# A gated mix of two attentions on one core: logits pieces of 512, 320, 320 and 128 columns in place of four of 320, a last Q part of 128 columns, a new order

## The chip, the core and the metric

The kernel runs on one core of one Trainium2 chip. Its five engines run at the same time and wait for each other by semaphores: TensorE (PE, matmuls, results into PSUM), VectorE (DVE), ScalarE (ACT), GpSimd (POOL) and SyncE (SP, which issues DMAs). PSUM has eight banks of 512 float32 columns on 128 partitions. The metric is the device time of the kernel in microseconds, lower is better.

## What is computed

The result is `g * a + (1 - g) * b`, with a gate `g` for each of 2,048 rows of x (512 columns, bfloat16).

```python
def _A_ref(x, mem0, Wq, Wk, Wv, Wo, seg_len):        # 32 heads of 128, seg_len 32, M = 8
    mem = mem0
    for s in range(n_seg):                           # 64 segments
        h = concatenate([mem, x[s * 32:(s + 1) * 32]])
        q, k, v = h @ Wq, h @ Wk, h @ Wv             # per head
        p = softmax(where(mask, q k^T * scale, -1e9))
        o = (p @ v) @ Wo
        mem = o[:, :M]                               # the next segment starts from it
        outs.append(o[:, M:])

def _B_ref(x, wq, wk, wv, wo, beta):                 # 32 heads of 16, 4 blocks of 512 rows
    for s in range(4):
        p = softmax(q[s] k[s]^T * scale + causal mask)
        o = sig(beta) * (phi(q[s]) M) / (phi(q[s]) z) + (1 - sig(beta)) * p @ v[s]
        M, z = M + phi(k[s])^T v[s], z + sum phi(k[s])
    return o @ wo

g = sigmoid((x * gate_w).sum(-1))
return g * _A_ref(...) + (1 - g) * _B_ref(...)
```

Attention A is a recurrence: the first eight output rows of a segment are the memory of the next one, so its 64 segments run one after the other. Attention B doesn't depend on A.

## The kernel before

**The whole.** The program first lists some 6,800 operations with their reads and writes and then lays them out on the engines. The order on each engine is written out: `ORDER` is a packed text that lists, for PE, ACT, DVE, POOL and SP, which operation comes when (`sequences`, L472; `given`, L396). Where an operation may run on one of two engines (copies out of PSUM on ACT or DVE, some products on DVE or POOL), the list on which it stands decides. Each operation's waits, and the PSUM banks that it gets, follow from the order.

**A segment of A** (`p_seg`, from L1444 on). The tokens and the memory, transposed, are projected with Wq, Wk and Wv (`wproj`, matmuls in L1422), each in two halves of 16 heads (r = 0 and 1). A projection's matmuls use all 128 rows of the array and 32 of its columns, so that four run side by side. Results are copied out of PSUM (`copy`, L1002), K and Q transposed on DVE (`ktr`, L1497). The second Q projection is made in two parts (`two`, L1555): a part's matmuls, its copy and its transposition follow each other. Then come the scores (L1512 and L1516; a mask matmul in L1029 before them), the exponential (L1521), the sums (L1536) and their reciprocals (L1540, L1542), the normalisation (L1544, L1546), and the value product of each half r (`f_pv`, L1577, and `f_pw`, L1586). A value product uses 32 rows and 128 columns of the array, four times side by side, and writes columns 0 to 159 of four PSUM banks, a *quad*. Copies take it to OT_sb, and Wo (L1314) makes the output rows and the memory of the next segment (DVE, L1332 to L1337). Rows whose result the next segment doesn't need are projected apart, four segments at once (`xr`, `rem_q`, `rem_k`, `rem_v`, `OTr_sb`), and fill TensorE between the steps of the recurrence.

**B in units.** B runs as 16 units, each of eight heads of a block of 512 rows, in two halves q = 0 and 1 of four heads. A half's logits, transposed and without the part above the diagonal, have 1,280 columns for each head: key blocks 0, 3, 1 and 2 with 512, 128, 384 and 256 columns, in that order (`COL`, L1123). They are made in four *pieces* of 320 columns (`PIECE`, L1125). A piece is one operation of TensorE (`p_logits`, matmuls in L1146, again 32 rows by 128 columns of the array, one matmul for each head and key block that it touches), two exponentials of ACT over two banks each (`p_exps`, L1164), and one mask of POOL over the 128 diagonal columns (L1170, `DIAG`). When all four pieces are done, the value product of B follows (L1187).

**Where the pieces stand.** From unit 3 on (`ALONE`), `plan` (L703) gives each of the 26 halves the segments between two rounded places of a straight line: they start in segments 1, 3, 5, 8, 10, 12, 15, 17, 20, 22, 24, 27, 29, 32, 34, 36, 39, 41, 43, 46, 48, 51, 53, 55, 58 and 60, and the last ends at 62. So 17 halves have two segments and nine have three. A piece either *rides*: it shares the quad of the second value product (r = 1) of a segment, in columns 160 to 479, and its matmuls come right before that product's (`carry`). Or it stands *alone*, with a quad of its own (`alone`, `p_piece`, L1193). Halves of two segments have two pieces alone, halves of three segments one. The pieces of units 0 to 2 all stand alone. A quad's banks are closed to others until all its copies and exponentials are done.

The lines that place them now:

```python
            for p, at in enumerate(((s - 0.3, s, s + 0.7, s + 1), (s, s + 0.7, s + 1, s + 2), (s, s + 1, s + 2, s + 3))[min(end - s, 4) - 2]):
                if at == int(at):
                    self.carry[int(at), 1] = (u, q, p)
                else:
                    self.alone.append((at, u, q, p))
```

Of the kernel before, what the change touches and what calls it, by code (L numbers as in the profile page):

```python
# [15 lines left out]
    "c-nPZ2|yIp8~@(U?#`aDpc0BE%HfgsomYk;kY(l-rCDN{VwqNIYMyCore%1Rnn!rynSz9h;(Z%lq-kEEsR;@!3(U@&|9i8?yczhf!tTy|^S$r*eZTK}Pd5Y_F;`It7Qt!M>jdXFZ"  # L16
    "o}-UlLQEyp%Znl@BL;{n;K2$&H>mTz4SFmT->}>Uj3k}Ax1#@|F)jy%a)CuJat}R+mVI0VSn<{jtTiAHr)-JHnVW?7+7^4Mjwxk0EEq7O){4P{F=1({YSvLVSQH!nLG4W_PiTg50"
    "2~?Cjevt%qpGqX9JTf2%N|n43{DSW=?CJH`$aW^l;(b7AT27at_>WV<G2E+e=NC_xT4})(%_O;1cK|@!%sMuR5FrosV`z$GZL-ngj8W-QHDeyQR&AmT>-AJX~r9w&EP<vf>k13>}"
    "YuMGWGzU!~8%&JQ-1f(c4LLI~N5IeQV0#?OF2!QE<RZ?L2efGsfP4iSf(uCn}cIN$12`{P+6F9gn+{LDZu1y+Cn%`e0KXaOQp5~=dwr?T)a2rjn0i#RdRP*D_60^lgLUW?-3T5AD"
    "jybi^^oj}%>U%zo>Jb8OZ<N}L1(=#JDDoS_`pkgh2B0%=U>r|~rbo`cqusO2TW~0a<WCe1=<RUh>xlYGAT@awnt*sMpDAF5er(SIgaCr*VEC!Gp!1GiZ{)5^AJm?7j_+?@1XVC66"  # L20
    "fK}v0dtnjOMt8&ES#TM#+-5CV24f)gF^mT=dd2_h7_tMPi`R}>Q*C+|IKc{F8M+b*CahBw{|@l86F&Jw<gJA$VEhbw5jb2flMdk9=>lxN@wK9KSIXHo05@sWTy_w|B0V@xG|X$k!"
    "5Qc(z>l4d0gO{L*8zySK|+AI=Yc|?i|A>-rv~5b&x$60G`~bF5g;`*UeUgp8#$P~WuO<H3;HrU6qp@?poi!G*1ZFJdo>Z@TR5FXf;4NkN4_;Q_>=tEN6g`@fLb1bpaQZOiBXA>+V"
    "H_fUo0j7tZRV`qWIE%l9QVe4i}WBen=dJJ$-3R$`vD)ECd(}i!6v}wbKMbU|KIybFj0I<yVs21`WWjcz74CIxX<zN6}V_>`=sknfI7Lom-iDQqlY4j3tj35S_u#NIL8@#(|@(^gD"
    "q0MO1`W<fvwgK|q|<WpWYQIAZErNVb+NA!hN)%6Z)m)oCLd#K2<P`G#<>Spirme1+>R!DTrEufjoS2e3LBmW(FSix)!Cv_)X{<k$nW+{BAwE4V<Gi@XNJ6qu-J|I%D~`W1pX(dr6"
    "(Zsdy$M1J#|UcaIjK_A87OP!BGmm~3{MiDW2`b1JS#zG4zYL8z&jn!$w&VgMtAR!PCfvr_vXm#I&D5^58Xr!WX?sD?;Wsu1EGvETU^t@Rm^QJ;WnomV`C2^nywC;mQ$Yfy?Ur|D_"
    "+x^7LIRr4fPb(%|7#Kycye@;J*805BKVblW2D^Y*GHwNd0uQboqwdro;&<wLP(!K-hDODb5;6!@=<%CuNDROMkMxyQ!@7G&;`g2uwoqyYIK2&-U4g}V{#iBP3SzT(=$yDIx0r};d"
    "Nfrr`}5L`NyOOQqQPFs*-F9YE_D=Av!#v~1t^1;Pt@?xMDN{1dK?MP(&QfgfDlfp4L48({ACl!_Z={bdSQl?kBP9gHeF!YDiZ}!fSaJ`F@)>OoG{{7l9QCr;5++xqT}nYJ(f%ef~"
    "c~)u+~#VO0>bU0*1m<2xW-kOk04bH`epzFFYc_HvHD-Ka11iv=>z?H<I=tQX?Qxb~61n`atq8hKl#IxN?r?i*2q4HEG5LAY^gk%flVv+w|Ack1N&eV+-P*$I%~$fqC(V=2F6+_tK"
    "`$8cX!18sAl7csb{#;Jk*=Paxt!Za1~P%cZhXN^zu1U15uA4^8D0gNtMmY~^4ON{QNWB&IM|jnZ6*Xhn-kCz4tQhr7rk=C+VQPuR<@C=B(ynW-%49~@;K9!UNyT@S$JF#tytozt5"
    "C5q%x@h_(LpPy`V@*Acw6w7TY-iq_!{C<tnj^Sg(%r<~diL6o##{=@EL37^jN263L+F9ox%n6xg^Gt&DDu=FUTEBz%LVBu$V;StF#Po6I_Sl#@!P^<e$H^}ZKKyE(N>>^7aeuavs"  # L30
    "k{{#SP{$7ig0u5Y#H#>}Wt<&{zDiRhT?0mtAHBEmPeKPL;WPxrHfu(gCf6ag`T(LL?1@J_fS6ROGaBXcH@L-8_<H^ipOtaX;r-0nFvbWeghvU(DST1;KExcXR$dh9w3HG@%d90<&"
    "ZW<b$c$)3=>3m_l&*Y%8{2^}?JvWB^OX~U;fkSdIUfR$4m;v2B`Bx%y#9>54MH3xB7MT$<H0T`m}T6&coXW6Tz;aqV#X!tpSC9S7t)}gBN}W{riGy>zgB*<TzR7uy-}OUuQyyO)-"
    "siOn$h@AL#ivGJ0EhjT1YoyYvW@MFLY>wp|);&Ib8AT;<D}gmu1TFWeRi2Xv>GoU=hpKt%IM&zyT+LjSMg{%J4pXZF;3H(_mrLFQqV+Mk!eItZb1NzWE}MK`K&_YyvM`A%AvKzYV"
    "6M0H<G6fTl+~AFZw|9zwo$KKdS=2?!i51O%%Fm0IS_mN~K|<SP-X20y3A9NgotFGgo9z#&ED)b^)HyWPWZdZABn)#r-7Kv>_;>|+c47YjIdg`vPoNGMcK=SH8l(t6$@=uwE7Cp>8"
    "J4G5f9fY3Gsdp_1c|2}SxF2o#+IoO!z`7&Dd$OV5rg4fas^_$65>v`>`tO75lLm)1OSd4-&iXHX_h^bH?qYv@SS-tpTj8@=i{0!Fx@dx;B>^y*$&Ibf2aaey?M-8ZvZ+2K906G;w"
    "WHuyZ#$|TBj5~wi3Yz~Vw*NjLKy;YPcpls)v}Wj_Jww``O8;rn?AhSbTfj}M4%p7)QNd<#1yT{P@4!jC%?t&m@28UsI&1?}pF;uNPRSB&F4OJ+^+iK~Symw&j*0|(Ke%>FY#=)BN"
    "0spfp&%?Kz=B6z9)ysf+03461+@^^-o}?i&M^U}c-C+77cFah+fy~TfT9r3H41Qh_k%GH?u0wY8qIIZc3Da0hh!jwt)LdMEzr%qwFd=0Yf$sPLpEI?83~L)1Ja1Ir4Am7O(Z5i7H"
    "sQrz;oYifr9W2n9Nw<l2@YM>RO+vTNqYiL!3<xQL)MTck{vq0&;jvo<Gh^0@8rGT41v2z;L1?*n+3d2;pr7mOweE(dIlIws*&e8XG)n-JF5!io%L><BK7Hv&ktcHjy~mb#d?~jV!"
    "hHj}G5V!QGw)64V9AOABTQzYPI(_@{P9>#MSPW`ymLx8jZ+ez)#j6d+sV=8A(zM$#eqPWZlF9-{?1D%y77{uvWcu*Wk2=1nIHIxroS<Q3gq^AiCitVL6|%S*}&loDNz?@|#Ovrg7"
    "tVs-B{y-BQ})dBi8M82qy(AlnBfoa~TlvstPHxaIbt8p>sJ>DE0b{9e41Ft?THB#-==UG!__3IXK+mmE1QP(Vx{pH-D1WKNm@Fcc2U4-G+QC{ppooCOXH7RU|H$SZ$i`v6)H=-7b"  # L40
    "VYu9TE#oa2e;Z&jsaRW&V{)EovUA||DA8f|LP&=Ln{Y%?&x_<KQD;2W0SBf{m_LaM<h6(5pzs2C2JQ12AqAhbglp-*#);na7n|lyhXr4N4HEHLgWwPD#SSD!HVDR{8{Tu6y*US{T"
    "kwLx);kMarJ>-i{{Z3k#8<PtesK_jfMBE~8$sYcJX(AOU-e^=7McSr$ZHXiS};|I!wb9Pdqj^{>_L5m!wW)1Ls6Lb%H0O&)dMxW-~+*eaNMm3PL2ezgRlUCx~tOTlSM@YAZOAy(+"
    "z^dU-Z??&t7;^!!dagxF)QSuheG>mt@P{{&6k&yP1Anj1uhzysfLXqOsecGwI$Kd#-IvuRHeD@OQnTYhdUyFp@WD)?z{RsFYnxlhNo;lcTNY6C1fJ96$HrHx0|rXq`8t&3>?OYX?"
# [93 lines left out]
class Slot(Res):  # L137
# [1510 lines left out]
```

## Time and profile before

| what | us |
|---|---|
| median of three runs | 815.55 (813.28 to 816.82) |
| the profiled execution | 813.89 |
| its span, first to last instruction | 811.9 |
| TensorE busy in the span | 788.2 |
| DVE, ACT, POOL busy | 643.7, 523.1, 257.8 |

How to read it: the span is what the profiler saw of one execution, and its own time lies 2.0 us above it. In the views, a line names the line of the program (L1146), the engine, the operation, the tiles it writes and reads (`pb` is PSUM), its size in partitions by elements, and a count (x4). PE is TensorE's matmuls, PEld its weight loads, which run beside them. Matmuls overlap, and their lengths are longer than the distance of their starts; what a piece of work costs TensorE is read from the start of one group to the start of the next. The mean granted clock of TensorE was 1.000.

### The profile page before, as it was taken

The numbers are of one execution on the slowest core, as the hardware profiler recorded it, in microseconds if no ns is written. First come the engines' busy times: TensorE is split into PE (matmuls) and PEld (weight loads), VectorE is DVE, ScalarE is ACT, GpSimd is POOL, SyncE is SP. The second block draws the span as 40 slices with busy tenths as digits, with TensorE's granted clock in tenths as the row PEclk, the third lists the DMA queues.
The fourth block names the chain that finished last, engine by engine and source line by source line (L and its number), as shares of the span: only waits on it lengthen the run. The fifth ranks groups of instructions, "written<-read, shape, count | busy, mean of one in ns | idle before, by whom it ended". The sixth has DMA issues, their size and how long they took to land.

```text
span 811.9 us, 51762 instructions
## 1 busy us (share of the span) xinstructions
PE 788.2 (97%) x23598; PEld 501.2 (62%) x23607; DVE 643.7 (79%) x1681; ACT 523.1 (64%) x1198; POOL 257.8 (32%) x564
## 2 busy tenths in 40 slices
PE   9899999999999999999999999999999999999987
PEld 4456666666666666666666665656766665666655
DVE  4878887788889787787787887786877898787886
ACT  4666656776666656767667666577666656766662
POOL 4542221233223332422422322333323223432440
PEclk9999999999999999999999999999999999999999
DMA  8983202121200111121011111100111010010001
GB/s 327 417 256 63 47 16 45 36 52 27 48 25 21 46 27 40 33 46 34 21 33 48 38 25 42 30 24 20 40 48 31 21 31 21 16 25 22 22 21 37
DMA packets 71696, 45.14 MB, mean 56 GB/s; under 512 B 50046, under 2 KB 69942, under 8 KB 69942
## 3 DMA queue, kind: packets, MB, share of 16 engines
q1 hardware_dynamic: 70422, 40.92, 17.8%
q8 instruction: 185, 3.03, 1.6%
q10 hardware_dynamic: 1056, 0.92, 0.4%
q14 instruction: 33, 0.27, 0.1%
HBM read 30.33 MB, written 8.87 MB: 48 GB/s over the span
## 4 chain that ended last, share of the span: by engine, by line
PE 84%; DVE 8%; DMA 3%; ACT 2%; issue 2%; SPq 1%; POOL 1%; DVEq 0%; POOLq 0%; ACTq 0%
PE pb L1422 46%; PE pb L1314 18%; PE pb L1029 6%; PE pb L1146 3%; PE pb L1187 2%; PE pb L1577 2%; DMA st<-in_gate_w_dram 2%; PE pb L1512 2%; PE pb L1536 1%; PE pb L1031 1%; DVE V_sb L1002 1%; PE pb L1586 1%; DVE st L1002 1%; PE pb L1235 1%; DVE QT_sb L1497 1%
## 5 line engine op out<-in xcount | busy, mean ns | idle before, releaser
L1164 ACT ACTIVATE PTB<-pb 128x640 bf16<-128x640 f32 x240 | 158.5, 705 | 41.0 <-PE pb L1146 29.8
L1002 ACT ACTIVATE st<-pb 128x512 bf16<-128x512 f32 (+2 forms) x232 | 112.9, 499 | 104.3 <-PE pb L1422 76.1
L1422 PE MATMUL pb<-Wv_sb,hT 128*32 128x512 bf16 x2048 | 152.5, 380 | 0.0
L1422 PE MATMUL pb<-Wq_sb,hT 128*32 128x256 bf16 (+1 forms) x3072 | 139.2, 308 | 0.3
L1314 PE MATMUL pb<-Wo_sb,OT_sb 128*32 128x256 bf16 x4096 | 130.8, 273 | 2.2 <-issue 1.8
L1422 PE MATMUL pb<-Wk_sb,hT 128*32 128x512 bf16 x2048 | 131.1, 379 | 1.2 <-issue 0.9
L1314 PEld LDWEIGHTS pb<-Wo_sb,OT_sb 128*32 128x32 bf16 x4096 | 102.3, 96 | 12.6 <-issue 2.3
L1170 POOL TENSOR_SCALAR_AFFINE_SELECT PTB<-PTB 128x512 bf16<-128x512 bf16 x120 | 77.7, 648 | 90.2 <-ACT PTB L1164 82.2
L1422 PEld LDWEIGHTS pb<-Wq_sb,hT 128*32 128x32 bf16 x3072 | 79.7, 97 | 42.4 <-DVE hT L1337 4.4
L1546 POOL TENSOR_TENSOR PT_sb<-PT_sb,rc_sb 128x64 bf16<-128x64 bf16 x81 | 28.9, 356 | 188.9 <-ACT rc_sb L1542 174.9
L1422 PEld LDWEIGHTS pb<-Wk_sb,hT 128*32 128x32 bf16 x2048 | 53.2, 97 | 49.6 <-DVE hT L1337 2.3
L1002 DVE CAST st<-pb 128x512 bf16<-128x512 f32 (+1 forms) x123 | 67.2, 549 | 15.4 <-PE pb L1422 12.7
L1002 ACT ACTIVATE OT_sb<-pb 128x320 bf16<-128x320 f32 (+1 forms) x139 | 57.4, 429 | 32.2 <-PE pb L1586 31.3
L1002 DVE CAST OT_sb<-pb 128x320 bf16<-128x320 f32 (+2 forms) x121 | 56.5, 475 | 18.5 <-PE pb L1586 17.6
L1002 DVE CAST V_sb<-pb 128x512 bf16<-128x512 f32 x90 | 61.5, 684 | 8.8 <-PE pb L1422 7.9
L1497 DVE STREAM_TRANSPOSE QT_sb<-st 128x128 f32<-128x128 f32 (+1 forms) x192 | 61.8, 335 | 8.3 <-ACT st L1002 6.4
L1540 ACT ACTIVATE rc_sb<-pb 128x160 f32<-128x160 f32 x128 | 38.9, 304 | 42.7 <-PE pb L1536 36.2
L1332 DVE STREAM_TRANSPOSE pb<-pb 128x256 f32<-128x256 f32 x63 | 29.3, 465 | 40.7 <-PE pb L1314 40.4
L1521 ACT ACTIVATE PT_sb<-pb 128x224 bf16<-128x224 f32 x128 | 45.5, 356 | 23.0 <-PE pb L1516 19.1
L1422 PEld LDWEIGHTS pb<-Wv_sb,hT 128*32 128x32 bf16 x2048 | 48.0, 97 | 20.0 <-ACT st L1002 0.7
L1497 DVE STREAM_TRANSPOSE KT_sb<-st 128x256 f32<-128x256 f32 x128 | 54.6, 427 | 7.0 <-ACT st L1002 5.5
L1544 DVE TENSOR_TENSOR PT_sb<-PT_sb,rc_sb 128x160 bf16<-128x160 bf16 x128 | 45.2, 353 | 8.9 <-ACT rc_sb L1542 7.3
(200 smaller groups left out, 1449.4 us busy)
## 6 DMA issues: line engine op xcount, KB each, us to landing
Wv_sb<-in_A_Wv_dram SPq DMA_DIRECT2D x4, 1024.0 KB, 11.2
Wk_sb<-in_A_Wk_dram SPq DMA_DIRECT2D x4, 1024.0 KB, 19.3
Wq_sb<-in_A_Wq_dram SPq DMA_DIRECT2D x4, 1024.0 KB, 26.6
Wo_sb<-in_A_Wo_dram SPq DMA_DIRECT2D x4, 1024.0 KB, 22.2
rest_v<-stg SPq DMA_DIRECT2D x112, 32.0 KB
rem_v<-rest_v SPq DMA_DIRECT2D x28, 128.0 KB, 2.5
a_rows<-ao SPq DMA_DIRECT2D x63, 32.0 KB
stg<-a_rows SPq DMA_DIRECT2D x15, 128.0 KB
```

Of the source, the lines that this page charges most:

```text
L1002: self.P.op(("act", "dve"), (lambda a: a.activation(dst, src(), ACT.Copy), lambda d: d.tensor_copy(dst, src())), reads=reads, writes=write ...
L1029: ins = pe.matmul(out[32 * c:32 * c + 32], lhsT[:, 32 * c:32 * c + 32], rhs, start=start, stop=stop, tile_position=(0, 32 * c), **kw)
L1164: P.op("act", (lambda dst=dst, src=src: lambda a: a.activation(dst, src(), ACT.Exp, scale=0.25))(), reads=[pair], writes=["%s%d_%d" % (nam ...
L1170: P.op("gp", (lambda pt=pt, ii=ii: (lambda g: g.affine_select(pt, pt, ([[0, len(ii)]] if len(ii) > 1 else []) + [[1, 128]], ALU.is_ge, 0.0 ...
L1314: ins = pe.matmul(pb[so.b][p0:p0 + 32, 0:256], tok(r, g, l), half(h, d, q), start=(r == 0 and g == 0 and l < 2), stop=(r == 1 and g == 3 a ...
L1332: P.op("dve", lambda d: d.transpose(pb[so.b][:, 256:512], pb[so.b][:, 0:256]), reads=[so], writes=[rt], name="turn%s" % name, cost=0.468, ...
L1422: ins = pe.matmul(self.pb[sl.b][32 * g:32 * g + 32, 0:hi - lo], x[:, c, 0:32], cols, start=(c == 0), stop=(c == C - 1), tile_position=(0, ...
L1497: op("dve", (lambda dst=dst, src=src: lambda d: d.transpose(dst, src))(), reads=["st%d%s" % (i, tag)], writes=["%sT%d%s" % (kind, r, tag)] ...
L1521: op("act", lambda a: a.activation(PT[:, r, :], pb[rb.b][:, 0:224], ACT.Exp, scale=SCALE), reads=[rb], writes=["PT%d" % r, "PT%dr" % r], n ...
L1540: op("act", lambda a: a.activation(rc[:, r, :], pb[rb.b][:, 0:160], ACT.Ln), reads=[rb], writes=[rr], name="ln%d_%d" % (s, r), cost=t_act( ...
L1544: op("dve", lambda d: d.tensor_tensor(mine[r], mine[r], by_head(rc[:, r, :]), ALU.mult), reads=[rp, rr], writes=[rp], name="nrm%d_%d" % (s ...
L1546: op(("dve", "gp"), tuple((lambda e: e.tensor_tensor(rest[r], rest[r], late(rc[:, r, :]), ALU.mult)) for _ in range(2)), reads=[rp + "r", rr],
```

## The change

Three things change.

First, the pieces. Their bounds now depend on how many segments the half has (`cut`). With two segments they are 0, 512, 640, 960 and 1,280, so pieces of 512, 128, 320 and 320 columns; with three segments 0, 352, 640, 960 and 1,280, so 352, 288, 320 and 320; otherwise four of 320. With two segments piece 0 (512 columns) stands alone ahead of segment s, piece 2 rides the second value product of s, piece 1 (128 columns) the first of s + 1 and piece 3 the second of s + 1. With three segments none stands alone: piece 0 (352) rides the second value product of s, piece 1 (288) the first of s + 1, piece 2 the second of s + 1 and piece 3 the second of s + 2. So 26 pieces fewer stand alone (17 in place of 43 from unit 3 on), and 26 first value products carry one. A piece of 352 columns fills its banks, 160 + 352 = 512.

Second, the second Q projection's parts are 384 and 128 columns in place of 256 and 256.

Third, `ORDER` is another text. Both texts list 6,790 operations: 2,979 on PE, 367 on SP; on ACT, DVE and POOL 1,203, 1,681 and 560 before and 1,177, 1,701 and 566 after.

```diff
-        self.carry, self.alone = {}, []
+        self.carry, self.alone, self.cut = {}, [], {}
...
-            for p, at in enumerate(((s - 0.3, s, s + 0.7, s + 1), (s, s + 0.7, s + 1, s + 2), (s, s + 1, s + 2, s + 3))[min(end - s, 4) - 2]):
-                if at == int(at):
-                    self.carry[int(at), 1] = (u, q, p)
-                else:
-                    self.alone.append((at, u, q, p))
+            self.cut[u, q] = k = min(end - s, 4) - 2
+            if not k:
+                self.alone.append((s - 0.3, u, q, 0))
+            for p, at in zip((0, 2, 1, 3), ((-1, 1, 2, 3), (1, 3, 2, 5), (1, 3, 5, 7))[k]):
+                if at > 0:
+                    self.carry[s + at // 2, at % 2] = (u, q, p)
...
-    PIECE = 320
+    PIECES = ((0, 512, 640, 960, 1280), (0, 352, 640, 960, 1280), (0, 320, 640, 960, 1280))
+
+    def piece(self, u, q, p):
+        at = self.PIECES[self.cut.get((u, q), 2)]
+        return at[p], at[p + 1]
...
-        P, pb, par, lo = self.P, self.pb, u % 2, self.PIECE * p
+        P, pb, par, (lo, hi) = self.P, self.pb, u % 2, self.piece(u, q, p)
...
-        parts = [(kc, max(lo, c0), min(lo + self.PIECE, c0 + 512 - 128 * kc)) for kc, c0 in self.COL.items()]
+        parts = [(kc, max(lo, c0), min(hi, c0 + 512 - 128 * kc)) for kc, c0 in self.COL.items()]
...
-        P, lo, n = self.P, self.PIECE * p, self.PIECE
+        P, (lo, hi) = self.P, self.piece(u, q, p)
+        n = hi - lo
...
-        two = ((0, 256), (256, 512))
+        two = ((0, 384), (384, 512))
```

More of the change, by code (lines that the diff above doesn't have):

```diff
@@ L20 @@
[L20 to L31, printed above, removed]
@@ L76 @@
[L76 to L79 removed]
+    "c-n1Q2S8Lu6P|t7xq~|dG1!QLC3Y-CVvAU?VTn;<iLrOZ5=+!*>@`ti#U72s-V0)HsMs|sQ4{^`6_9cV+`Zj@_r1G&<v@YEd%Lq!zWHWm*%HDR+I2ea6IZD7&kPvJ&7Q)I4shWGf"
@@ L1148, in f_l @@
             return ins
-        o = P.op("pe", f_l, reads=["KT8_%d" % par, "QTm" if q else "QT8_%d" % par], writes=slot.pairs, name="bL%d_%d" % (u, 4 * q + p), cost=0.15,
+        o = P.op("pe", f_l, reads=["KT8_%d" % par, "QTm" if q else "QT8_%d" % par], writes=slot.pairs, name="bL%d_%d" % (u, 4 * q + p), cost=0.017 + (hi - lo) / 2400,
                  prio=prio, mode="r32")
```

115 lines of the change are left out of this document (63 added, 52 removed).

## The prediction

> **What bounds the kernel now.** I read the page's busy shares first, then the shares of the chain of waits by engine, then the busy time of the stretch without start and end.
>
> ```profile
> span 811.9 us, 51762 instructions
> PE 788.2 (97%) x23598; PEld 501.2 (62%) x23607; DVE 643.7 (79%) x1681; ACT 523.1 (64%) x1198; POOL 257.8 (32%) x564
> ...
> PE 84%; DVE 8%; DMA 3%; ACT 2%; issue 2%; SPq 1%; POOL 1%; DVEq 0%; POOLq 0%; ACTq 0%
> ```
>
> ```profile
> 68.00:780.00 712.00, 700.31 (x21618) 452.07 (x21614) 574.43 (x1504) 471.53 (x1090) 220.63 (x470) 1.00 0.14 33
> ```
>
> TensorE (PE) sets the time: it holds 84% of the chain, and from 68 to 780 us it idles 11.7 of 712 us at full granted clock. So a gain must come from TensorE time itself, and TensorE can be busy on the page while it only changes from one kind of matmul to another. That is read from starts in the timeline. First the undisturbed pace, in the timeline of TensorE alone (start, length, and what):
>
> ```profile
> 383.34 1.04 PE L1422 MATMUL pb<-Wq_sb,hT 128*32 128x512 bf16 x16
> 384.20 1.90 PE L1422 MATMUL pb<-Wk_sb,hT 128*32 128x512 bf16 x32
> 385.93 0.28 PE L1422 MATMUL pb<-Wq_sb,hT 128*32 128x256 bf16 x4
> ```
>
> ```profile
> 404.07 1.93 PE L1314 MATMUL pb<-Wo_sb,OT_sb 128*32 128x256 bf16 x64
> 405.83 0.39 PE L1422 MATMUL pb<-Wq_sb,xr 128*32 128x512 bf16 x4
> ```
>
> Four matmuls run side by side, one for each 32 columns of the array. 32 of 512 columns take 385.93 - 384.20 = 1.73 us, so a group of four takes 0.216 us; 64 of 256 columns take 1.76 us, 0.110 us a group. A column costs 0.216/512 = 0.42 ns.
>
> **The change part by part: pieces that stand alone.** A logits piece has another shape, 32 rows by 128 columns of the array, as have the value products (L1577, L1586); everything around them is 128 by 32. A piece alone looks like this:
>
> ```profile
> 540.20 0.39 PE L1422 MATMUL pb<-Wk_sb,xr 128*32 128x512 bf16 x4
> 540.52 0.32 PE L1146 MATMUL pb<-QT,KT 16*128 16x320 bf16 x4
> 540.77 0.62 PE L1422 MATMUL pb<-Wk_sb,xr 128*32 128x512 bf16 x8
> 541.21 0.60 PE L1422 MATMUL pb<-Wq_sb,hT 128*32 128x512 bf16 x8
> ```
>
> From 540.20 to 541.21 are 1.01 us. The three groups of 512 columns in it are worth 3 x 0.216 = 0.65, so the piece costs 0.36 us, though its 320 columns are worth 0.135. The rest, 0.225, is change of shape: 540.52 - 540.20 - 0.216 = 0.10 going in, 0.25 - 0.135 = 0.11 coming out, 0.01 in the group after. The Trainium skill, "TensorEngine Tiling (Array Packing)", section Key Properties, says that a change of tiling mode drains the array, and "TensorE: Matmul & The Clock Gate", Step-by-step, step 4, puts a drain at about 128 cycles of 2.4 GHz, 53 ns. By these an estimate for 26 visits with two drains each would be 2.8 us; by the rows it is 5.9, and the rows decide.
>
> Now a value product without a piece, and one with a piece riding:
>
> ```profile
> 389.39 0.61 PE L1422 MATMUL pb<-Wv_sb,hT 128*32 128x512 bf16 x8
> 389.93 0.27 PE L1577 MATMUL pb<-PT_sb,V_sb 32*128 32x40 bf16 x16
> 390.06 0.21 PE L1586 MATMUL pb<-PT_sb,rem_v 32*128 32x64 bf16 x4
> 390.20 0.40 PE L1422 MATMUL pb<-Wv_sb,hT 128*32 128x512 bf16 x4
> 390.42 0.39 PE L1314 MATMUL pb<-Wo_sb,OTr_sb 128*32 128x256 bf16 x8
> ...
> 391.07 0.39 PE L1314 MATMUL pb<-Wo_sb,OT_sb 128*32 128x256 bf16 x8
> 391.40 0.32 PE L1146 MATMUL pb<-QTm,KT 32*128 32x64 bf16 x8
> 391.55 0.26 PE L1577 MATMUL pb<-PT_sb,V_sb 32*128 32x40 bf16 x16
> 391.65 0.19 PE L1586 MATMUL pb<-PT_sb,rem_v 32*128 32x64 bf16 x4
> 391.77 0.84 PE L1314 MATMUL pb<-Wo_sb,OT_sb 128*32 128x256 bf16 x24
> 392.44 0.28 PE L1314 MATMUL pb<-Wo_sb,OTr_sb 128*32 128x256 bf16 x4
> ```
>
> Without: 390.42 - 389.39 = 1.03, less three groups of 512 (0.65), is 0.38 us. With: 392.44 - 391.07 = 1.37, less eight groups of 256 (0.88), is 0.49. So 320 riding columns cost 0.11 us, 0.025 less than their columns (the value product's own start, 391.55 to 391.65, is quicker behind them than 389.93 to 390.06). For other widths I move this by 0.42 ns a column: 128 columns 0.03, 288 columns 0.10, 352 columns 0.12, and alone 512 columns 0.36 + 0.08 = 0.44.
>
> The places follow from the plan. The 26 half units from unit 3 on start in segments 1, 3, 5, 8, ... 62; 17 of them last two segments, nine last three. A two-segment half has two pieces alone and two riding now, 2 x 0.36 + 2 x 0.11 = 0.94; changed, one of 512 alone, 128 riding a first value product and two of 320 as now: 0.44 + 0.03 + 0.22 = 0.69. It saves 0.25. A three-segment half has 0.36 + 3 x 0.11 = 0.69 now and 0.12 + 0.10 + 0.22 = 0.44 changed, and saves 0.25. Sum: 26 x 0.25 = **6.5 us**. The lower bound of this term is 0 (a new order that sets the riding piece apart from its value product keeps the change of shape). The upper bound is 26 x 0.36 = 9.4, a moved piece for nothing.
>
> The columns stay 1,280 a half. There are 68 fewer matmuls of the 768 in L1146; a group of 40 columns takes (391.65 - 391.55)/4 = 0.025 us where its columns are worth 0.017, so 17 groups fewer give under 0.2 us: nothing.
>
> **The exponentials** stay two instructions a piece.
>
> ```profile
> L1164 ACT ACTIVATE PTB<-pb 128x640 bf16<-128x640 f32 x240 | 158.5, 705 | 41.0 <-PE pb L1146 29.8 <-DVE OT_sb L1002 9.1
> L1002 ACT ACTIVATE st<-pb 128x512 bf16<-128x512 f32 x126 | 75.2, 598 | 69.2 <-PE pb L1422 65.8 <-PE pb L1029 2.4
> L1002 ACT ACTIVATE st<-pb 128x256 bf16<-128x256 f32 x71 | 27.0, 383 | 15.6 <-PE pb L1422 10.4 <-DVE ao L1345 4.2 <-PE pb L1029 0.6
> ```
>
> (598 - 383)/256 = 0.84 ns an element. A piece of 128 columns over two banks needs 0.38 us an instruction, 288 columns 0.65, 512 columns 0.705 + 0.32 = 1.03. Per two-segment half 2 x (1.03 + 0.38 + 0.705 + 0.705) = 5.64 us, the same as 8 x 0.705. ACT is busy 64%, so the amount costs nothing; the place matters. In 26 segments 0.77 or 1.30 us of ACT work now comes behind the first value product, and until it ends that product's four PSUM banks stay closed. In TensorE's own queue the first value products and all later work stand behind the riding piece, but those products needed the same four banks anyhow. The mask on POOL is one for each piece as before; SyncE's list keeps its 367 entries, so no DMA is added.
>
> **The last Q part.** The second Q projection is cut 384 + 128 in place of 256 + 256, with the same columns for TensorE.
>
> ```profile
> L1497 DVE STREAM_TRANSPOSE QT_sb<-st 128x128 f32<-128x128 f32 x128 | 34.9, 285 | 2.8 <-ACT st L1002 1.9
> L1497 DVE STREAM_TRANSPOSE QT_sb<-st 128x256 f32<-128x256 f32 x64 | 27.8, 434 | 5.5 <-ACT st L1002 4.4
> ```
>
> ```profile
> PEld pb L1512 <- DVE QT_sb L1497: 3.7, 13, 0.5
> ```
>
> By slopes (0.84 ns above, (434 - 285)/128 = 1.16 ns here) the last part's eviction falls from 383 to 275 ns and its transposition from 285 to 211: 0.18 us less behind the last Q matmul. The first part gets 0.18 us longer and is ready 128 columns later; if nothing stands between the parts it becomes the late one: matmuls 4 x 0.162 = 0.65, eviction 0.49, transposition 0.36, then the second transposition 0.21, together 1.71 us against 0.87 + 0.38 + 0.29 = 1.54 now. So per segment it lies between -0.18 and +0.17. TensorE feels it only where the scores wait: the weight loads of L1512 waited 13 times, 3.7 us. Bounds: -3.7 us (all these waits gone) and 13 x 0.17 = +2.2. I take -0.4, near nothing, since at least 51 of 64 segments hide it behind other matmuls.
>
> **The new order.** It has 6,790 entries as before; 26 leave ACT, DVE gains 20, POOL six. That is at worst 20 evictions of 512 columns on DVE, 20 x 0.68 = 13.6 us.
>
> ```profile
> L1002 DVE CAST st<-pb 128x512 bf16<-128x512 f32 x66 | 44.5, 675 | 9.6 <-PE pb L1422 8.5 <-PE pb L1029 0.3
> ```
>
> DVE goes from 79% to (643.7 + 13.6)/805 = 82%, hidden behind TensorE; without that cover it would cost up to the 13.6 us. What else the order moves the trace cannot show; its bounds are the middle's idle time, 11.7 us to gain, and the rival below to lose. I take 0, because it has to place the same matmuls as now.
>
> **Sum:** -6.5 - 0.4 = -6.9 us. The profiled execution took 813.89 us (span 811.9 and 2.0 around it), so 807.0. The median of the runs shown, 815.55, lies 1.66 above it: 808.6, call it **808.5 us**.
>
> **Rivals.** First, *PSUM banks at the first value product*, which ends slower. Its price from rows:
>
> ```profile
> 226.38 0.68 DVE L1002 CAST V_sb<-pb 128x512 bf16<-128x512 f32 x1
> ...
> 226.52 0.21 PE L1586 MATMUL pb<-PT_sb,rem_v 32*128 32x64 bf16 x4
> ...
> 227.12 0.32 PE L1146 MATMUL pb<-QTm,KT 32*128 32x64 bf16 x8 [0.39 <-DVE V_sb L1002]
> ```
>
> ```profile
> 390.34 0.77 ACT L1002 ACTIVATE OT_sb<-pb 128x320 bf16<-128x320 f32 x2
> ```
>
> At 227.12 TensorE stood idle 0.39 us before a riding piece until DVE had emptied the V bank: four free banks are already scarce there. In the segment at 389.93 the first product's banks are empty at 390.34 + 0.77 = 391.11, and the second product opens its own four at 391.40. With a riding piece of 128 columns the first four come free at 391.88, 0.48 late; with 288 columns at 392.41, 1.01 late. In full that is 17 x 0.48 + 9 x 1.01 = 17.2 us: 807.0 + 17.2 + 1.7 = 825.9. The Trainium skill, "TensorEngine Tiling (Array Packing)", section Gotcha 1: PSUM Pressure, says the same in general, that row tiles writing to different banks raise the pressure on PSUM; the 0.39 us agrees. Against it: eight banks hold both quads, TensorE has other projections to put in between, and 26 separate openings of four banks go away. It eats the gain at 6.9/26 = 0.27 us a visit, and costs half a per cent at 0.42.
>
> Second, *half given back or nothing done*: half of that price, 8.6 us, ends at 817.3; a new order that leaves the 26 visits separate ends at about 815.5. For it: the waits above. Against it: the riding piece is written directly ahead of its value product.
>
> Third, *the order also removes idle time*: half of the middle's 11.7 us gives 808.5 - 5.9 = 802.6. For it: scores and value products each wait for evictions that the order moves. Against it: these waits are spread over many short places.
>
> **How the numbers follow.** Forecast 0.50, with its own range 804 to 811.5 from the Q bounds (-3.3 and +2.6 around its term, and the rest of the 6.5); third rival 0.14; second 0.20; first 0.16. Half a per cent, 4.1 us, is what a measurement of this kernel tells from no change (its runs lie 813.28 to 816.82), so faster means below 811.5 and slower above 819.6. Faster: nearly all of the forecast, 0.47, and the third, 0.14: 0.61. Same: the second and the forecast's rest, 0.22 with a margin. Slower: 0.17. The range 801.5 to 819 leaves out the first rival and the lowest of the third.
>
> **What would show it.** In the changed profile L1146 has 700 matmuls; pieces between two groups of 128 by 32 matmuls number 17 from unit 3 on, with 0.10 and 0.11 us around each; first value products that carry a piece follow it within 0.1 us. Idle before L1146 or L1577 at these 26 places beyond 0.27 us a visit would make the forecast wrong, as would a busy TensorE of 788 us unchanged. The waits of L1512 for QT_sb should stay between 0 and 6 us.

## The result, and the profile after

The changed kernel takes 824.49 us (median of four, 823.63 to 827.59) against 815.28 us in the same session: a ratio of 1.0118, with a 95% interval of 1.0095 to 1.0140. It is slower by 9.2 us, where 808.5 was forecast.

The page of the changed kernel, its span, busy shares and the shares of the chain of waits by engine:

```profile
span 822.4 us, 51755 instructions
...
PE 793.8 (97%) x23602; PEld 485.7 (59%) x23602; DVE 654.2 (80%) x1701; ACT 518.3 (63%) x1172; POOL 260.1 (32%) x570
...
PE 83%; DVE 8%; DMA 3%; ACT 2%; issue 2%; SPq 2%; POOL 0%; DVEq 0%; POOLq 0%
```

Its busy time by stretches (columns: stretch, length, busy PE, PEld, DVE, ACT and POOL, granted clock, DMA share, GB/s):

```profile
68.00:780.00 712.00, 697.66 (x21462) 434.86 (x21454) 578.87 (x1508) 461.53 (x1056) 220.91 (x472) 1.00 0.14 33
780.00:823.00 43.00, 35.34 (x1009) 20.99 (x1005) 32.37 (x83) 17.18 (x43) 9.69 (x22) 0.94 0.10 28
...
801.00:804.50 3.50, 3.50 (x64) 2.15 (x60) 1.54 (x5) 0.00 (x0) 0.75 (x2) 0.54 0.00 0
```

In the middle TensorE does 156 matmuls less than before in the same 712 us and idles 14.3 us instead of 11.7. At 801 us its granted clock is about half for 3.5 us, worth some 1.6 us in this execution: 3.5 x (1 - 0.54). The end of the kernel before ran at full clock. That is not the loss, though: of the four runs of the changed kernel one had a mean granted clock of 1.000, and it took 823.63 us.

The pieces themselves do what was forecast. A piece of 128 columns that rides with a first value product, in the timeline of TensorE:

```profile
396.02 0.61 PE L1428 MATMUL pb<-Wv_sb,hT 128*32 128x512 bf16 x8
396.56 0.23 PE L1151 MATMUL pb<-QTm,KT 32*128 32x128 bf16 x4
396.63 0.26 PE L1583 MATMUL pb<-PT_sb,V_sb 32*128 32x40 bf16 x16
396.73 0.19 PE L1592 MATMUL pb<-PT_sb,rem_v 32*128 32x64 bf16 x4
396.86 0.40 PE L1428 MATMUL pb<-Wv_sb,hT 128*32 128x512 bf16 x4
```

The value product starts 0.07 us behind the piece. Over the whole trace, too, the prices are those of the prediction, by medians: 0.43 us for a piece of 512 columns alone (forecast 0.44), and 0.41, 0.49 and 0.50 us for a value product with 128, 288 and 352 columns riding (forecast 0.41, 0.48 and 0.50). The 17 lone pieces are there, and 24 of the 26 new riding pieces stand directly ahead of a first value product; the other two (at 706 and 728 us) stand by themselves. Ahead of these 26 pieces and of the products directly behind them TensorE is idle 0.01 us in all by the profile, where the prediction had named 0.27 us a visit as a sign that it is wrong.

Other signs did turn against it. TensorE's busy time rose from 788.2 to 793.8 us, and the weight loads of the changed kernel wait longer (columns: what waited, for what, us in total, times, longest):

```profile
PEld pb L1518 <- DVE QT_sb L1503: 6.2, 20, 0.7
PEld pb L1518 <- DVE KT_sb L1503: 5.5, 19, 0.8
...
PEld pb L1428 <- DMA rest_v<-stg: 2.6, 6, 0.8
PEld pb L1428 <- DMA out_dram<-stg: 2.5, 1, 2.5
```

The other waits of these kinds before, beside the 3.7 us for QT_sb that the prediction shows:

```profile
PEld pb L1512 <- DVE KT_sb L1497: 2.5, 9, 0.5
...
PEld pb L1422 <- DMA rest_v<-stg: 0.8, 2, 0.6
```

The scores wait 11.7 us instead of 6.2 (for QT_sb alone 6.2 us, where the prediction allowed up to 6). Projections wait 5.1 us instead of 0.8 until a DMA has emptied a staging tile, which is a buffer (`stg`) in which rows wait for their store.

**An account of all runs.** From the starts of TensorE's groups I split the time from the end of segment 1 to the end of segment 62 (the writes of hT) in three: columns at 0.42 ns (a small group by its usual spacing); change of shape, which is up to 0.115 us beyond the columns where the shape changes; and idle, the rest. Each line is one profiled execution. How small groups are priced moves the level of the idle column by 2 to 3 us, for all kernels alike; the differences between kernels hardly move.

```
us                          segment 1   1 to 62   columns   change of shape   idle
before                           58.1     725.3     659.2              34.4   31.7
e1  before, reordered            70.7     728.4     659.6              34.4   34.3
e3  Q part alone                 71.3     726.5     659.6              34.2   32.8
e5  e1 with old start            59.6     728.3     658.2              34.4   35.6
e13 before, stores first         57.8     728.8     660.1              34.4   34.3
changed                          61.2     730.2     659.6              29.5   41.1
e2  changed, reordered           60.9     725.3     659.1              29.6   36.6
e4  pieces alone                 67.3     725.9     659.1              29.3   37.5
e6  changed with old start       59.0     729.8     658.9              29.9   41.1
e7  both, old start              58.2     723.6     658.5              29.8   35.2
e8  pieces alone, old start      59.3     731.5     659.4              29.4   42.7
e9  changed, one store moved     59.9     727.0     659.9              29.6   37.5
e12 e7, stores first             59.4     724.0     659.3              29.9   34.7
e14 planned with slow DVE        59.6     726.4     659.1              30.1   37.0
e15 before, no lone pieces       57.8     720.0     653.5              25.4   41.0
e16 changed, no lone pieces      60.9     730.8     655.1              25.9   49.9
```

Over the whole program TensorE's visits to the other shape fall from 186 to 165, by 21 and not by the 26 of the prediction. 21 x 0.225 = 4.7 us is close to what "change of shape" loses (34.4 to 29.5). It comes back as idle time, and more with it: idle rises by 9.4 us.

### The profile page after: what moved, and what is told of

It reads as the page before. It is cut to its first block, busy times and chain, and to the rows that moved or that the text cites. A ratio compares the mean times of both kernels' runs of the same rounds, so it can differ in the third digit from the quotient of the medians.

```text
span 822.4 us, 51755 instructions
## 1 busy us (share of the span) xinstructions
PE 793.8 (97%) x23602; PEld 485.7 (59%) x23602; DVE 654.2 (80%) x1701; ACT 518.3 (63%) x1172; POOL 260.1 (32%) x570
## 4 chain that ended last, share of the span: by engine, by line
PE 83%; DVE 8%; DMA 3%; ACT 2%; issue 2%; SPq 2%; POOL 0%; DVEq 0%; POOLq 0%
PE pb L1428 46%; PE pb L1320 17%; PE pb L1030 6%; PE pb L1151 3%; PE pb L1193 2%; PE pb L1583 2%; PE pb L1518 2%; DMA st<-in_gate_w_dram 2%; PE pb L1542 2%; PE pb L1032 1%; DVE st L1003 1%; DVE V_sb L1003 1%; PE pb L1592 1%; DVE OT_sb L1003 1%; DVE ao L1351 1%
## 5 line engine op out<-in xcount | busy, mean ns | idle before, releaser
L1003 ACT ACTIVATE st<-pb 128x512 bf16<-128x512 f32 (+3 forms) x236 | 119.3, 512 | 116.5 <-PE pb L1428 84.5
L1170 ACT ACTIVATE PTB<-pb 128x640 bf16<-128x640 f32 (+2 forms) x240 | 158.7, 704 | 35.4 <-PE pb L1151 23.7
L1428 PE MATMUL pb<-Wq_sb,hT 128*32 128x512 bf16 (+2 forms) x3072 | 142.1, 308 | 1.3 <-DVE hT L1343 0.4
L1320 PE MATMUL pb<-Wo_sb,OT_sb 128*32 128x256 bf16 x4096 | 137.8, 275 | 0.8 <-ACT OT_sb L1003 0.2
L1428 PEld LDWEIGHTS pb<-Wq_sb,hT 128*32 128x32 bf16 x3072 | 72.5, 97 | 52.8 <-DVE hT L1343 5.2
L1003 DVE CAST OT_sb<-pb 128x320 bf16<-128x320 f32 (+1 forms) x133 | 61.9, 473 | 24.7 <-PE pb L1592 23.7
L1003 ACT ACTIVATE OT_sb<-pb 128x320 bf16<-128x320 f32 (+1 forms) x127 | 53.4, 431 | 38.5 <-PE pb L1592 37.0
L1003 DVE CAST V_sb<-pb 128x512 bf16<-128x512 f32 x100 | 68.3, 683 | 9.1 <-PE pb L1428 7.6
L1003 DVE CAST st<-pb 128x512 bf16<-128x512 f32 (+2 forms) x112 | 58.4, 527 | 9.9 <-PE pb L1428 7.6
L1503 DVE STREAM_TRANSPOSE QT_sb<-st 128x192 f32<-128x192 f32 (+2 forms) x192 | 61.4, 334 | 4.7 <-ACT st L1003 2.0
L1550 DVE TENSOR_TENSOR PT_sb<-PT_sb,rc_sb 128x160 bf16<-128x160 bf16 x128 | 47.0, 367 | 10.1 <-ACT rc_sb L1548 9.2
```

The lines of the kernel that those rows point to most:

```text
L1003: self.P.op(("act", "dve"), (lambda a: a.activation(dst, src(), ACT.Copy), lambda d: d.tensor_copy(dst, src())), reads=reads, writes=write ...
L1170: P.op("act", (lambda dst=dst, src=src: lambda a: a.activation(dst, src(), ACT.Exp, scale=0.25))(), reads=[pair], writes=["%s%d_%d" % (nam ...
L1320: ins = pe.matmul(pb[so.b][p0:p0 + 32, 0:256], tok(r, g, l), half(h, d, q), start=(r == 0 and g == 0 and l < 2), stop=(r == 1 and g == 3 a ...
L1428: ins = pe.matmul(self.pb[sl.b][32 * g:32 * g + 32, 0:hi - lo], x[:, c, 0:32], cols, start=(c == 0), stop=(c == C - 1), tile_position=(0, ...
L1503: op("dve", (lambda dst=dst, src=src: lambda d: d.transpose(dst, src))(), reads=["st%d%s" % (i, tag)], writes=["%sT%d%s" % (kind, r, tag)] ...
L1550: op("dve", lambda d: d.tensor_tensor(mine[r], mine[r], by_head(rc[:, r, :]), ALU.mult), reads=[rp, rr], writes=[rp], name="nrm%d_%d" % (s ...
```

## The experiments

The order on an engine is a list, and the kernel's own planner (`given`, which also hands out the PSUM banks) says how long a list should take: 801.02 us for the order before, 800.93 for the new one. So the two orders are equals on paper. New orders were made from them by many small random moves that keep this length; a ratio is always to the kernel before, run on the same chip.

**Other orders, and each part alone (e1 to e4).**

```diff
 e1: before.py    -ORDER = (text)          +ORDER = (another text, planned 801.05)
 e2: after.py     -ORDER = (text)          +ORDER = (another text, planned 800.89)
 e3: before.py    -two = ((0, 256), (256, 512))   +two = ((0, 384), (384, 512)), order planned 802.05
 e4: after.py     -two = ((0, 384), (384, 512))   +two = ((0, 256), (256, 512)), order planned 802.43
```

> The program before with nothing changed but the packed order: pieces of 320 columns and a Q part of 256 as before, the same matmuls, another order whose length by the kernel's own planner is the same (801.05 us against 801.02). The order theory (the loss comes from how the new order meets the chip, not from the pieces or the Q part): the time moves by more than 3 us against 815.3, most likely upwards, 818 to 826. The pieces theory and the Q theory (the loss hangs on one of the two changes of structure): 815.3 within 2 us.

> The changed program with nothing changed but the packed order; its length by the kernel's own planner is 800.89 us against 800.93. The order theory: the time moves by more than 3 us against 824.5, to either side. The pieces theory and the Q theory: 824.5 within 2 us, since pieces and Q part are those of the changed kernel.

> The kernel before with the Q part of 384 and 128 columns alone; pieces of 320 columns as before, the order worked over until its planned length is 802.05 us, 1 us more than before. The Q theory (scores wait longer for the wide part): 823 to 826, with the waits of the scores for QT_sb at 6 us against 3.7. The pieces theory: 815 to 818. The order theory: 816 to 826, with waits spread over scores, rest projections and start-up rather than at QT_sb alone.

> The changed kernel with the Q part put back to 256 and 256 columns; the pieces as in the changed kernel, the order worked over until its planned length is 802.43 us, 1.5 us more. The pieces theory (the first value product waits for the banks and exponentials of the piece that rides with it): 824 to 828. The Q theory: 815 to 818. The order theory: 816 to 828, and the idle time just ahead of the first value products under 5 us more than before, so that the loss lies elsewhere.

Measured: e1 830.51 us (ratio 1.0198, 1.0161 to 1.0235), e2 819.17 (1.0057, 1.0032 to 1.0081), e3 827.40 (1.0161, 1.0124 to 1.0198), e4 823.77 (1.0114, 1.0080 to 1.0149). With nothing but the order exchanged, the program before loses 16 us and the changed program gains 5. That is the order theory, and in e1 by more than it had said (818 to 826). The losses of e1, e3 and e4 lie mostly in the start, by the weight loads' longest waits, first e1, then e3, then e4:

```profile
PEld pb L781 <- DVE xT L913: 12.5, 2, 12.2
```

```profile
PEld pb L1008 <- POOL ident L787: 12.6, 1, 12.6
...
PEld pb L1503 <- DVE QT_sb L1488: 4.6, 17, 0.6
PEld pb L1503 <- DVE KT_sb L1488: 2.5, 9, 0.5
```

```profile
PEld pb L1023 <- DVE xT L914: 8.6, 1, 8.6
...
PEld pb L1509 <- DVE QT_sb L1494: 5.7, 21, 0.7
PEld pb L1509 <- DVE KT_sb L1494: 4.4, 14, 0.6
```

By the end of segment 1 these three are 9 to 13 us behind the kernel before (see the account), and the planner does not foresee it: most of that is one wait in the first 20 us, while the weights are loaded. Behind it the clock is low as well, in e1 0.93 on average over the first 70 us against 1.00 before; what share of the loss that is was not separated. e3 and e4 therefore say little by their times, but their score waits do: 7.1 us with the new Q part alone (e3), 10.1 with the new pieces alone (e4), 11.7 with both and 6.2 with neither. The longer score waits come with the pieces. What the Q part adds, about one, is no more than kernels with the old pieces differ by among themselves (6.2 to 7.4).

**The start put back (e5 to e8).**

```diff
 e5: e1           -start of e1             +first 58 us of the plan in the order of before
 e6: after.py     -start of the new order  +first 62 us in the order of before, order from 130 us on kept
 e7: after.py     -ORDER                   +first 62 us in the order of before, then e2's order worked over
 e8: e4           -ORDER                   +first 62 us in the order of before, then e4's order worked over
```

> e1_before_reordered (the program before, another order of the same planned length, 830.5 us) with the first 58 planned microseconds put back to the order of before, the rest as in e1; planned length 801.09 us. The order theory, with the loss of e1 sitting in its start (it reaches the end of segment 1 at 70.7 us against 58.1 before): 817 to 820. Rival, the loss is spread over the later order: 826 or more.

> The changed kernel, pieces and Q part as they are, with the first 62 planned microseconds put to the order of before and the order behind 130 us left as in the changed kernel; planned length 801.52 us, 0.6 more. If the start of the new order is worth what the traces differ by at the end of segment 1 (61.2 against 58.1 us): 821 to 823, so most of the loss stays. Rival, the start is the cause: 816 or less. Rival, the start of before does not carry over: 824 to 826.

> The changed program, pieces and Q part as they are, with the start of before and the later order of e2_after_reordered worked over (planned length 801.19 us). The order theory: the changed structure with neither the start nor the middle of the new order runs at 814 to 818, the loss of 9 us gone. The pieces theory and the Q theory: 821 to 825, since pieces and Q part are there.

> The pieces alone (Q part of 256 and 256), with the start of before and the later order of e4_pieces_alone worked over (planned length 801.61 us). The order theory: 813 to 817, since e4's later order lost 6 us to its plan behind the start. The pieces theory: 820 to 825. By the traces of the first four runs the pieces are worth 2 us after all, 4.9 saved in changes of shape and 3 given back in waits of the scores, so that this run against e5_before_reordered_old_start should come out 1 to 4 us lower.

Measured: e5 819.55 (1.0056, 1.0026 to 1.0087), e6 823.29 (1.0102, 1.0083 to 1.0121), e7 815.48 (1.0001, 0.9987 to 1.0016), e8 822.11 (1.0089, 1.0066 to 1.0111). e5 gets back 11 of the 16 us that e1 lost, so these lay in the start. e7 has every part of the change but the new order and runs as fast as the kernel before: the loss of 9 us is the order's, not the structure's. e6 shows that the start holds only about one of the nine. By the account e6 and e7 differ by 6.2 us between segments 1 and 62, and nearly all of it is idle time (41.1 and 35.2). e8 missed the forecast of the order theory (813 to 817) and lies in the range of the pieces theory (820 to 825), 2.6 us above e5, its counterpart with the old pieces. Its order lost 42.7 us idle, and its longest waits are spread over scores (9.9 us) and staging tiles (3.0); no single cause was found. e7 shows that the new pieces don't have to cost this much, but e8 leaves open how much of it is theirs.

**One store moved (e9).** The timeline of the changed kernel at its longest single wait behind the start:

```profile
275.05 1.27 SPq L1089 DMA_TRANSPOSE stg<-KT  x1
...
275.47 0.75 DVE L1295 SCALAR_TENSOR_TENSOR stg<-pb,omg_sb,t_sb 128x512 bf16<-128x512 f32 x1
...
276.95 0.44 SPq L987 DMA_DIRECT2D wvB_sb<-in_B_wv_dram  x1
277.44 0.85 SPq L987 DMA_DIRECT2D wqB_sb<-in_B_wq_dram  x1
278.33 0.51 SPq L1297 DMA_DIRECT2D out_dram<-stg  x1
282.39 1.05 PE L1428 MATMUL pb<-Wk_sb,xr 128*32 128x512 bf16 x16 [2.19 <-DMA out_dram<-stg]
```

The output tile is ready at 275.47 + 0.75 = 276.22, but SyncE issues two weight loads first, and the store leaves at 278.33. A rest projection (Wk, for the rows whose result the next segment doesn't need) wants that staging tile, and TensorE stands still 2.19 us.

```diff
 SP, entries of the new order:
+    dma_out3
     dma_wvB8
     dma_wqB9
-    dma_out3
```

> The changed kernel with one entry of the order moved: on SyncE the store of the fourth output tile goes ahead of two weight loads (wvB, wqB) instead of behind them. In the trace of the changed kernel its tile is finished at 276.2 us, the store is issued at 278.33 us behind the two loads, which take 1.4 us, and a rest projection waits 2.19 us for it at 282.39 us, in the stretch of segments 19 and 20 that takes 26.2 us against 22.4 before. If that queue is what the wait is made of: the wait falls to about 0.8 us, the stretch to about 24.8 us, the time by 1 to 1.5 us to about 823. Rival, the wait stands for something else: stretch and time unchanged, 26.2 and 824.5.

Measured: 819.34 us (1.0053, 1.0034 to 1.0071), five less than the changed kernel, for one entry of 6,790, where 1 to 1.5 us had been expected. The same place in e9:

```profile
273.50 0.75 DVE L1286 SCALAR_TENSOR_TENSOR stg<-pb,omg_sb,t_sb 128x512 bf16<-128x512 f32 x1
...
274.99 0.44 SPq L1288 DMA_DIRECT2D out_dram<-stg  x1
275.47 0.83 SPq L978 DMA_DIRECT2D wvB_sb<-in_B_wv_dram  x1
276.34 0.57 SPq L978 DMA_DIRECT2D wqB_sb<-in_B_wq_dram  x1
278.07 1.04 PE L1419 MATMUL pb<-Wk_sb,xr 128*32 128x512 bf16 x16
```

The wait is gone. Segment 20 takes 11.23 us instead of 13.56, so 2.3 us are located here. The profiles also differ by 1.3 us in the start, which is untouched, and by 1.1 us in the end (25.9 instead of 27.0 us from the end of segment 62 to the last matmul), where the changed kernel's execution had its half clock and e9's had none. Where the medians' five us come from beyond these 2.3 was not settled.

**The price of the banks (e10).**

```diff
+        k = 32 if p == 1 and self.cut.get((u, q), 2) < 2 else n
...
-                dst, src = t[:, :, lo:lo + n], lambda pair=pair: self.pp[pair.b // 2][:, :].rearrange("p (k x) -> p k x", k=2)[:, :, base:base + n]
+                dst, src = t[:, :, lo:lo + k], lambda pair=pair: self.pp[pair.b // 2][:, :].rearrange("p (k x) -> p k x", k=2)[:, :, base:base + k]
...
```

> The changed kernel, order and all, with the exponentials of the 26 pieces that ride with a first value product cut to their first 32 columns of 128 or 288, so that the quad of banks is given back by ScalarE up to 0.4 us sooner at 17 of them and 1 us sooner at 9; the other columns of these pieces are left out of the result. The theory of banks at the first value product (priced at 17.2 us in full, 0.27 us a visit to lose what the pieces save): 808 to 816. The order theory: the places that lose are elsewhere (start, rest projections, scores, end), so 821 to 824.5, the small gain from ScalarE's lighter load.

Measured: 824.95 us (1.0132, 1.0087 to 1.0178), no gain. The first rival of the prediction had named 825.9 us, and the changed kernel came out near it by luck: its mechanism has no part in it. The 0.01 us of idle time at these places says the same.

**Stores first everywhere (e11 to e13), and a planner that knows of a slower VectorE (e14).**

```diff
 e11: after.py   SP list: 50 entries moved, stores ahead of the loads and row stores that stood before them
 e12: e7         SP list: 56 entries likewise
 e13: before.py  SP list: 53 entries likewise
 e14: after.py   order behind 62 us planned with other prices (804.21 by the kernel's planner)
```

> The changed kernel with 50 entries of SyncE's order moved: every store out of a staging tile behind 62 us goes ahead of the loads and row stores that stood between it and the end of the work that filled its tile, wherever the planned length stays at 800.93 us; the other four engines' orders are untouched. If the middle of the new order loses its time to staging tiles that come free late (5 us of waits for DMA in the changed kernel, 0.8 before): 816 to 819, at or below e9_store_first's 819.3, and waits for DMA under 2 us. Rival, e9's single store was the only one that mattered: 819 to 820. Rival, the moved row stores and loads become late in their turn: above 821.

> e7_both_old_start (815.5 us) with the same rule, 56 entries of SyncE moved, planned length unchanged at 801.19 us. Its waits for DMA in the middle are 3 us, of which some two thirds should be on the path: 812.5 to 814.5, below both kernels. Rival, the waits are hidden or the rule makes others late: 815 to 817.

> The kernel before with the same rule, 53 entries of SyncE moved, planned length unchanged at 801.02 us. It waits 1.4 us for DMA behind its start in all, so if these waits are the mechanism there is little to win: 814 to 816. Rival, the rule helps or hurts through something else (the order in which transfers share the queues): more than 2 us off 815.4 to either side.

> The changed program with the start of before and a later order worked over with a planner that lengthens VectorE's all-SBUF instructions beside GpSimd by a quarter of the overlap, gives stores 0.3 us more and applies the clock rule to the end; by the kernel's own planner it is 804.21 us long, 3 us more than e7. If VectorE's longer instructions beside GpSimd (8 to 9 us in the changed kernel, 6 before) are a second part of what orders lose on the chip: 812 to 815, the loss to the plan behind the start under 4 us. Rival, they are mostly hidden: 817 to 819, the 3 us of the longer plan.

Measured: e11 821.90 (1.0088, 1.0052 to 1.0124), e12 **812.33** (0.9965, 0.9948 to 0.9982), e13 815.28 (1.0000, 0.9979 to 1.0020), e14 815.65 (1.0003, 0.9988 to 1.0018). e12 is faster than both kernels, by 2.8 us against before. Its waits for DMA ahead of weight loads, behind the start, where e7 had 1.7 us for rest_v alone:

```profile
PEld pb L1418 <- DMA rest_v<-stg: 0.9, 2, 0.5
...
PEld pb L1582 <- DMA rem_v<-rest_v: 0.3, 1, 0.3
```

They fell by 0.5 us, which is less than the gain, and the traces can't show the rest: the profiled execution of e12 happened to take 814.73 us and that of e7 812.97, the other way round than their medians. So the gain is measured, and its place is not shown. e13 is the control: an order with few such waits gains nothing. e11 missed its forecast. Its waits for staging tiles fell from 5.1 to 1.4 us, but it is no better than e9, the intervals overlap, and against e9 its trace loses 2.8 us between segments 32 and 42; 0.7 us of that is a wait for row loads. The line for the whole of e11, where e9 has 0.3 us:

```profile
PE pb L1583 <- DMA rem_v<-rest_v: 1.2, 2, 0.7
```

So the rule is not free: what is moved back can be late in its turn, as the rival above 821 us had it. e14 came out between its two forecasts, 3 us longer on paper than e7 and no slower, which fits VectorE's slower instructions as a part of the loss and does not show it.

**Lone pieces left out (e15, e16).**

```diff
+        alone = u >= self.ALONE and (u, q, p) not in self.carry.values()
         def f_l(pe):
             ins = None
+            if alone:
+                for i in range(4):
+                    ins = pe.matmul(pb[slot.banks[i]][32 * i:32 * i + 32, base:base + 8], self.ones[:, 0:32],
+                                    self.ones[:, 0:8], start=True, stop=True, tile_position=(0, 32 * i))
+                return ins
...
-            P.op("act", ... a.activation(dst, src(), ACT.Exp, scale=0.25) ...
+            P.op("act", ... a.activation(dst, src(), ACT.Exp, scale=0.001 if alone else 0.25) ...
```

> The kernel before, order untouched, with the matmuls of the 43 pieces that stand alone from unit 3 on left out: in their place stand four matmuls of 8 columns in the shape of the work around, so that both the columns and the two changes of shape go (and the logits of these pieces with them; their exponentials stay, over what lies in the banks). By the prediction's step a visit costs 0.36 us on the path, and all of it is won: 43 x 0.34 = 14.6 us, 801. If, as the score waits of the new-piece kernels say, TensorE work at these places partly covers the waits of scores and other chains, a good part comes back as idle time: 5 to 10 us won, 805 to 810, with more idle time ahead of the scores.

> The same in the changed kernel, order untouched: 17 pieces of 512 columns stand alone from unit 3 on, 0.44 us each by the prediction's rows. All on the path: 17 x 0.42 = 7.1 us, 817. If these places partly cover waits: 2 to 5 us won, 819.5 to 822.5.

Measured: e15 811.26 us (0.9950, 0.9923 to 0.9977), 3.7 us won of 14.6 (1.9 to 6.3 by the interval); e16 823.15 (1.0096, 1.0069 to 1.0122), 1.3 of 7.1, which is within the noise against the changed kernel. Both are less than even the second expectation said (5 to 10 and 2 to 5 us). The account of e15 shows both sides: columns and change of shape fall by 5.7 + 9.0 = 14.7 us, just as the prediction priced them, and idle rises by 9.3. The wait that grows most is that of the first projections for hT, the memory that one segment hands to the next, and not, as expected, that of the scores; first before, then e15:

```profile
PEld pb L1422 <- DVE hT L1337: 6.7, 20, 0.9
```

```profile
PEld pb L1430 <- DVE hT L1345: 15.7, 39, 0.9
```

A lone piece is filler: TensorE does it while the chain of the segment (attention, its output, hT, the next projections) runs on other engines. Take it away and TensorE comes sooner to a segment that is not ready.

The change itself moves pieces and doesn't remove them, and there the time comes back elsewhere. Its wait for hT is no longer than before; what grows are the waits of the scores and for staging tiles:

```profile
PEld pb L1428 <- DVE hT L1343: 6.5, 19, 0.9
```

## Why the prediction was wrong

- **Pieces that stand alone, -6.5 us.** The prices of a visit were right (0.36 us alone; by these rows 14.6 us for the 43 of e15, and 14.7 measured), and nearly all the places: 700 matmuls in L1151, 24 of 26 pieces directly ahead of their value products. The count was too high, 26 visits fewer where 21 went, so that the change of shape gave 4.9 us and not 5.9. The step that failed is that all of it is on the path. e15 says that a lone piece's time is worth 3.7/43 = 0.09 us, not 0.34, since most of it covers waits. The other runs bear that out. From the mean of the five kernels with all the old pieces to that of the eleven with all the new ones (e10 and e11 with 40.9 and 39.9 us of idle time among them), change of shape falls from 34.4 to 29.6 us and idle rises from 33.7 to 38.6. Some 3 to 4 us of that rise stand ahead of the scores: 6.2 to 7.4 us of waits for QT_sb and KT_sb with the old pieces, 9.3 to 12.5 with the new. The orders spread widely around these means: the best (e7, e12) pass from segment 1 to 62 in 1.7 and 1.3 us less than the kernel before, so what the pieces are worth under the best order of each structure stays open. The prediction read "PE 84% of the chain" and 1.6% idle as a TensorE with nothing in front of it; the idle time was small because filler stood there. (It also lets the halves start in segments up to 62; by the plan the last starts in 60 and ends at 62. No number hangs on that.)
- **The last Q part, -0.4 us.** In e3 the scores wait 7.1 us against 6.2 to 7.4 in the other kernels with old pieces, inside the bounds of -3.7 and +2.2. The durations were right:

```profile
L1503 DVE STREAM_TRANSPOSE QT_sb<-st 128x192 f32<-128x192 f32 x64 | 22.8, 356 | 1.2
...
L1503 DVE STREAM_TRANSPOSE QT_sb<-st 128x64 f32<-128x64 f32 x64 | 13.8, 216 | 0.4
```

  356 and 216 ns were forecast as 0.36 and 0.21 us. No run measures the time of this part by itself.
- **The new order, 0.** This is the step that made the loss. It was taken at 0 "because it has to place the same matmuls as now", but matmuls are not what an order costs. The structure of the change with another order runs at 815.5 us (e7), so the new order costs 9 us against that one. The prediction had bounded the order's gain, by 11.7 us of idle time, but for its loss it pointed to the rival on banks, which did not happen. Located are about 1 us in the start (e6), 2.3 us at one store behind two weight loads (e9), and in the profiled execution some 1.6 us of half clock at the end. The rest, about half, is spread over waits of scores and rest projections, and why this order meets them more often than e7's stays open.
- **The rivals.** Banks at the first value product: refuted by e10 and by the 0.01 us of idle time there. Half given back: right in kind, for the pieces, but through the segment's chain and the scores. The order as a rival was drawn only as a gain; as a loss it was missing.

## What to carry to other kernels

A TensorE that is 97% busy may still be waiting for a recurrence, with filler in the gaps: price a saving there by leaving the work out once (here 3.7 us for 14.7 us of work), not by its length. An order written out by hand or by a planner is a part of the change with a price of its own, here from -3 to +16 us at about equal planned length; compare a change of structure under more than one order. On an issuing engine that works its list in order, a store that frees a buffer may belong ahead of a load that is needed later, as long as that load has time: that took 5 us off here once (e9) and 3 us once (e12), nothing in e13, and in e11 no more than the one store of e9 had.

## What was not expected of the hardware

**The clock.** Before the stretch of 0.54 clock at 801 us TensorE had not been idle long; the windows ahead of it:

```profile
798.00:801.00 3.00, 1.71 (x72) 1.34 (x70) 2.68 (x6) 1.58 (x5) 1.88 (x4) 0.97 0.03 8
```

It was busy 1.71 of these 3.00 us, in pieces, with no wait longer than 0.5 us, and the clock fell all the same. The Trainium skill, "TensorE: Matmul & The Clock Gate", section What's actually happening, lets the clock fall after at least one idle window of some 3.4 us. The trace agrees with the length (3.5 us) but not with the condition: the window was partly busy.

**VectorE beside GpSimd.** The timeline of the changed kernel, and the mean of that instruction:

```profile
277.17 0.63 POOL L1176 TENSOR_SCALAR_AFFINE_SELECT PTB<-PTB 128x512 bf16<-128x512 bf16 x1
277.25 0.73 DVE L1550 TENSOR_TENSOR PT_sb<-PT_sb,rc_sb 128x160 bf16<-128x160 bf16 x1
```

```profile
L1550 DVE TENSOR_TENSOR PT_sb<-PT_sb,rc_sb 128x160 bf16<-128x160 bf16 x128 | 47.0, 367 | 10.1 <-ACT rc_sb L1548 9.2
```

The normalisation of a value product took 730 ns instead of 367 on average, and a mask had started on GpSimd 0.08 us before it. In this trace none of the 33 such instructions with nothing beside them on GpSimd takes over 327 ns, and the four longest, 726 to 883 ns, all have GpSimd work that started less than 0.1 us before them. The Trainium skill, "SBUF — State Buffer", section Who interferes with whom, says that the two share a pair of ports and the later one waits. The trace agrees that the later one is held up, but the instruction ends 0.18 us after the mask, sooner than if none of its work had been done beside it.

**A store's landing.** From the end of its issue (278.33 + 0.51) to the matmul that it released are 3.55 us, where the kernel's planner counts 2.2 from there. Two weight loads had been issued just ahead of it; whether they made the difference was not tested.
